# Decode layer on one core: a 128-row block of w4 moved to 16 partitions, its other rows in loads of 5, 4, 3 and 1

## The chip, the cores and the metric

The kernel runs on one NeuronCore of a Trainium2 chip. The metric is the device time of one execution in microseconds (us), the median over three runs; lower is better. All times in the text are microseconds unless marked ns. Positions such as 185.53 are counted from the start of the profiled span.

## The reference, cut to what matters

Eight tokens (B = 8, one step each, D = 512) go through two stages.

```python
# A: pre-norm attention, 32 query heads on 8 key/value heads, last W = 2048 cache positions
q = (layernorm(x) @ wq).reshape(B, 1, 32, 128)
p = softmax(q @ k_cache[:, :, -2048:].T * 128**-0.5)
h = x + (p @ v_cache[:, :, -2048:]).reshape(B, 1, 4096) @ wo
# B: on layernorm(h); the token shift is zero for one step, so only the MLP is left
x1 = layernorm(h)
h2 = h + x1 + gelu(layernorm(x1) @ w3) @ w4      # w3: 512 x 1792, w4: 1792 x 512
```

All inputs are bf16. The cache slices are 64 MiB, wq and wo 4 MiB each, w3 and w4 1.75 MiB each: the kernel reads 79.18 MB (million bytes) from HBM.

## The kernel before, in words

Every large load is issued by SyncE (SP) into one queue, in an order written out by hand: wq, 32 cache loads of 2 MB (16 for k, 16 for v) into the eight slots of `ring`, four loads of wo (1 MB each) into `wbig`, two of w3, four of w4. A cache load waits (on SP) until its slot is free: `taken[...]` is the last PE product that reads the slot. w3 goes to slot 0 and w4 to slot 1 of the ring. Each of these loads fills 128 partitions, one piece of memory per partition.

For each of the eight tokens and two halves of the heads, PE transposes the keys (L325), ScalarE and VectorE copy them out (L334, L336), PE makes the scores (L345), a softmax follows, and PE multiplies with the values (L445, L454). GpSimd (POOL) spreads the softmax over four head columns (L384). The attention output is reordered (L534 to L540) and multiplied by wo in four parts as the loads land (`pe_wo`, L548). `hd` (L685), the statistics (L687 to L699) and `uT` (L692) lead to the MLP.

The MLP works on 14 chunks of 128 rows of the hidden width. `pe_w3(half, ...)` (L710) makes `y_ps` in two halves of the contraction, one for each load of w3. VectorE scales it into `g_x` (L738), ScalarE makes `gT` by gelu (L741), in two groups of chunks: the first `FH` = 8, then 6. `pe_fin` (L747) starts the sum in `z_ps` with the residual, and `pe_w4` (L755) adds two products of 256 columns for each chunk, one for each half of the output, waiting for the load of w4 that holds the chunk:

```python
FH = 8
for r, sem in zip((8, 3, 2, 1), sem_w4):
    w4_chunks += [slice(f0 + i, f0 + 128 * r, r) for i in range(r)]
    dma(SP, w4_sb[:, lo:lo + r, :].rearrange("p r n -> p (r n)"),
        B_w4[f0:f0 + 128 * r, :].rearrange("(p r) n -> p (r n)", r=r), sem, w_free[1] if lo == 0 else None)
```

So a load with r rows per partition gives r chunks, and its wait stands ahead of the products of these chunks. Two copies out of `z_ps` (L775, L776) and the store (L779) end the program.

`stream(n)` puts n products of 512 columns on PE whose result nobody reads (L596); they stand between stages from the last values on. There are 21 of them: 4, 3, then 0, 4, 4, 1 behind the four parts of wo, then 2, 1 and 2.

Of the kernel before, what the change touches and what calls it, by code (L numbers as in the profile page):

```python
# [11 lines left out]
B = 8  # L12
D = 512
# [9 lines left out]
FC = F // 128  # L23
# [3 lines left out]
NS = 8  # L27
# [40 lines left out]
def bass_sequential_preLN__sliding_block_cached__mixer_s_mlp__decode_kernel(  # L68
# [23 lines left out]
    with es:  # L92
        sb = lambda shape, dtype, name: es.enter_context(nc.sbuf_tensor(name, shape, dtype))
        ps_t = lambda shape, dtype, name: es.enter_context(nc.psum_tensor(name, shape, dtype))
        S = lambda name: es.enter_context(nc.semaphore(name))
# [4 lines left out]
        ident_b = sb([128, 128], dt.bfloat16, "ident_b")  # L100
# [16 lines left out]
        QH, RW = H // 8, 8  # L117
# [4 lines left out]
        ring = sb([128, NS, NCQ * DH], dt.bfloat16, "ring")  # L122
        W3S, W4S = (2 * 2 * NB) % NS, (2 * 2 * NB + 1) % NS
        w3_sb = ring[:, W3S, 0:KC * F].rearrange("p (k f) -> p k f", k=KC)
        w4_sb = ring[:, W4S, 0:FC * D].rearrange("p (k n) -> p k n", k=FC)
# [4 lines left out]
        P4_sb = sb([128, 512, 4], dt.bfloat16, "P4_sb")  # L130
# [42 lines left out]
        gT = sb([128, FC * B], dt.bfloat16, "gT")  # L173
# [6 lines left out]
        kbank = [t[:, :].bitcast(dt.float32) for t in kT_ps]  # L180
# [10 lines left out]
        sem_wo = [S(f"sem_wo{i}") for i in range(NWO)]  # L191
        sem_x, sem_wq, sem_out = (S(n) for n in ("sem_x", "sem_wq", "sem_out"))
        sem_w3 = [S(f"sem_w3{i}") for i in range(2)]
        sem_w4 = [S(f"sem_w4{i}") for i in range(4)]
        PE, AC, DV, PO, SP = (Engine(S(n)) for n in ("s_pe", "s_act", "s_dve", "s_pool", "s_sp"))

        def dma(eng, dst, src, sem, *waits):
            def f(e):
                e.dma_start(dst, src).then_inc(sem, 16)  # L199
            eng.op(f, *waits, inc=False)  # L200
# [18 lines left out]
        e = DV.op(lambda e: e.bn_stats(st6[:, :], x_sb[:, :]), X)  # L219
        e = DV.op(lambda e: e.bn_aggr(mv[:, :], st6[:, :]), e)  # L220
        e = AC.op(lambda e: e.activation(rstd[:, :], mv[:, 1:2], ACT.Sqrt, bias=eps1[0:B, :], scale=1.0), e, e_eps)
        e = DV.op(lambda e: e.reciprocal(rstd[:, :], rstd[:, :]), e)
# [36 lines left out]
        e = PE.op(pe_xT, e_xln, e_idb)  # L259
# [22 lines left out]
        e = PE.op(pe_qT, *e_qr)  # L282
# [18 lines left out]
        place = {l: n for n, l in enumerate(quads)}  # L301
        taken = {}
# [6 lines left out]
        e_sp, e_max, e_mT, e_neg, e_negps, e_negc, e_exp, e_PT, e_pT, e_lsel, e_Lb, e_rL, e_scale = ({} for _ in range(13))  # L309
        NG = NB * 8  # L310
        NV = 2 * NB - 1
        LAST = NB - 1
# [174 lines left out]
        def pick_rest(w, *parts):  # L487
            for a in parts:
                pick_part(w, a, DV)
                if a == 3:  # L490
                    e_acc[w] = e_part[w]
# [51 lines left out]
        def pe_wo(n, *waits):  # L543
            def f(e):
                for q in range(n * (QH // NWO), (n + 1) * (QH // NWO)):
                    for r in range(RW):
                        for nb in range(KC):
                            ins = e.matmul(hT_ps[:, nb * NW:(nb + 1) * NW], wo_v[:, q, r, cols[nb]],  # L548
                                           oR_t[:, r * NW + q * B:(r + 1) * NW + q * B], start=(q == 0 and r == 0 and nb == 0),
                                           stop=(q == QH - 1 and r == RW - 1), skip_group_check=True)  # L550
                return ins
            e_wo.append(PE.op(f, (sem_wo[n], 16), e_exp[NB - 2], *waits))
# [4 lines left out]
        def pv(*quarters):  # L557
            for i in quarters:
                pe_PV(i)
                if i in at:  # L560
                    finish(at[i])
                if i == NG - 1:
                    scale(LAST, 1, S_ps[1][:, 0:16], e_PV[i])
# [29 lines left out]
        def stream(n):  # L593
            def f(e):
                for _ in range(n):
                    ins = e.matmul(O2_ps[:, :], ident_b[:, :], kT_sb[:, (NG - 1) % NKT, 0:512], start=True, stop=True)  # L596
                return ins
            if n:
                PE.op(f, e_acc[NV - 4])
# [37 lines left out]
        pick_rest(14, 1)  # L637
        finish(13)
        pick_rest(14, 2, 3)
        stream(4)  # L640
        pv(60)
        finish(14)
        pv(61, 62, 63)

        e_oR = reorder()
        stream(3)
        for n in range(NWO):
            pe_wo(n, e_oR, e_oz)
            stream((0, 4, 4, 1)[n])


        dma(SP, wq_v, A_wq.rearrange("(p k) n -> p k n", k=KC), sem_wq)
        for l in loads:
            what, b, j = l
            if what == "wo":
                n, qh = b, QH // NWO
# [4 lines left out]
            n = place[l]  # L661
# [4 lines left out]


        w_free = [taken[quads[n - NS]] for n in (len(quads), len(quads) + 1)]
        for a, sem in enumerate(sem_w3):
            dma(SP, w3_sb[:, 2 * a:2 * (a + 1), :].rearrange("p r f -> p (r f)"),  # L670
                B_w3[256 * a:256 * (a + 1), :].rearrange("(p r) f -> p (r f)", r=2), sem, w_free[0])

        FH = 8
        w4_chunks, w4_ends, f0 = [], [], 0
        for r, sem in zip((8, 3, 2, 1), sem_w4):
            lo = len(w4_chunks)
            w4_chunks += [slice(f0 + i, f0 + 128 * r, r) for i in range(r)]
            dma(SP, w4_sb[:, lo:lo + r, :].rearrange("p r n -> p (r n)"),
                B_w4[f0:f0 + 128 * r, :].rearrange("(p r) n -> p (r n)", r=r), sem, w_free[1] if lo == 0 else None)
            w4_ends.append(lo + r)  # L680
            f0 += 128 * r
        assert len(w4_chunks) == FC

        e_uz = PO.op(lambda e: e.memset(uT, 0.0), e_PT[LAST, 3])
        e_d = DV.op(lambda e: e.tensor_tensor(v3(hd[:, :]), hT, v3(xc[:, :]), ALU.add), e_wo[-1], e_xc[0])  # L685
# [5 lines left out]
        e_ms = DV.op(lambda e: e.tensor_reduce(msum[:, :], vr(st1), AX.X, ALU.add), e_st1)  # L691
        e_u = DV.op(lambda e: e.scalar_tensor_tensor(uT[:, :, 0:B], bc(msum), -1.0 / D, v3(hd[:, :]),  # L692
                                                     ALU.mult, ALU.add), e_ms, e_uz)
        stream(2)
        e_vs = DV.op(lambda e: e.tensor_reduce(vsum[:, :], vr(st2), AX.X, ALU.add), e_st2)
        e_m2 = DV.op(lambda e: e.tensor_tensor(msq[:, :], msum[:, :], msum[:, :], ALU.mult))
        e_vs = DV.op(lambda e: e.scalar_tensor_tensor(vsum[:, :], msq[:, :], -1.0 / D, vsum[:, :],
# [7 lines left out]
        def pe_w3(half, lo, hi, *waits):  # L705
            def f(e):
                for fc in range(lo, hi):
                    n, f = divmod(fc, FH)
                    for kc in (2 * half, 2 * half + 1):
                        ins = e.matmul(y_ps[n][:, f * NY[n]:(f + 1) * NY[n]], w3_sb[:, kc, w4_chunks[fc]],  # L710
                                       uT[:, kc, 0:NY[n]], start=(kc == 0 and f == 0), stop=(kc == KC - 1),
                                       skip_group_check=True)
                return ins
            return PE.op(f, *waits)
        pe_w3(0, 0, FC, e_u, (sem_w3[0], 16), e_scale[LAST, 1], e_acc[NV - 2])
        stream(1)
        e_y = [pe_w3(1, 0, FH, (sem_w3[1], 16)), pe_w3(1, FH, FC)]

        e = AC.op(lambda e: e.activation(s2[:, :], vsum[:, :], ACT.Sqrt, bias=eps2[:, :], scale=(1.0 + EPS) / D), e_vs)  # L719
        e1 = AC.op(lambda e: e.activation(s1[:, :], vsum[:, :], ACT.Sqrt, bias=eps1[:, :], scale=1.0 / D))  # L720
# [2 lines left out]
        e = DV.op(lambda e: e.reciprocal(r1[:, :], s1[:, :]), e1)  # L723
        e = DV.op(lambda e: e.tensor_tensor(v3(xb[:, :]), v3(hc[:, :]), bc(r1), ALU.mult), e, e_hc)
        e = DV.op(lambda e: e.tensor_tensor(xb[:, :], xb[:, :], hp[:, :], ALU.add), e)
        e = DV.op(lambda e: e.tensor_tensor(v3(fin[:, :]), hT, v3(xb[:, :]), ALU.add), e)
        e = DV.op(lambda e: e.tensor_copy(f_hi[:, :], fin[:, :]), e)
# [6 lines left out]
        e_gT = []  # L734
        for n in range(2):
            fn = (FH, FC - FH)[n]
            cs = slice(n * FH * B, (n * FH + fn) * B)
            e = DV.op(lambda e, n=n, cs=cs, fn=fn: e.tensor_tensor(v3(g_x[:, cs]),   # L738
                y_ps[n][:, 0:fn * NY[n]].rearrange("p (f w) -> p f w", w=NY[n])[:, :, 0:B], bcf(r2, fn),
                                                                   ALU.mult), e_y[n], e_r2)  # L740
            e_gT.append(AC.op(lambda e, cs=cs: e.activation(gT[:, cs], g_x[:, cs], ACT.Gelu_apprx_tanh), e))  # L741
        z_ps = S_ps[1]

        def rows(e, w, rhs, start=False, stop=False):
# [3 lines left out]
                               stop=stop, tile_position=(0, 64 * a), skip_group_check=True)  # L748
            return ins

        def pe_w4(lo, hi, *waits):
            def f(e):
                for fc in range(lo, hi):
                    for a in range(2):
                        ins = e.matmul(z_ps[64 * a:64 * a + B, 0:256], gT[:, fc * B:(fc + 1) * B],  # L755
                                       w4_sb[:, fc, 256 * a:256 * (a + 1)].rearrange("p (j r) -> p r j", r=2),
                                       start=False, stop=(fc == FC - 1), tile_position=(0, 64 * a), skip_group_check=True)
                return ins
            return PE.op(f, *waits)

# [4 lines left out]
            return ins  # L765

        PE.op(pe_fin, e_fin, e_exp[LAST], e_scale[LAST, 1])
        stream(2)
        for n, hi in enumerate(w4_ends):
            e_z = pe_w4(w4_ends[n - 1] if n else 0, hi, (sem_w4[n], 16), e_gT[0 if hi <= FH else 1])  # L770
        e_out = []
        for a in range(2):
            src = z_ps[64 * a:64 * a + B, 0:256].rearrange("p (r j) -> p r j", r=2)
            dst = out_sb[:, 256 * a:256 * (a + 1)].rearrange("p (j r) -> p r j", r=2)
# [38 lines left out]
```

## Time and profile before

| | us |
|---|---|
| median of 3 runs (193.53 to 193.57) | 193.54 |
| the profiled execution | 193.76 |
| its span, first to last instruction | 192.3 |
| PE busy | 159.8 |
| VectorE busy | 103.8 |
| ScalarE busy | 84.4 |
| GpSimd busy | 35.8 |

The profiled execution lies 0.22 above the median, and 1.46 of it lies outside the span. The granted TensorE clock of the core is 1.000. The instruction trace names the line, the tiles and the releaser of a wait; for the loads it also holds each packet (start, duration, bytes, queue) and the landing events of each load, one from each DMA engine that carried a part of it. The packets are not marked with their engine.

### The profile page before, as it was taken

To read this page: it belongs to the slowest core of one execution; us is meant where nothing else is said; L and a number is where in the kernel's file an instruction comes from. 1 tells how busy PE (TensorE), PEld (TensorE's weight loads), DVE (VectorE), ACT (ScalarE), POOL (GpSimd) and SP (SyncE) were. 2 spreads that over 40 slices of the span, in tenths; PEclk is the share of its full clock that TensorE was granted. 3 is DMA by queue.
4 is the path that set the end of the run, shared out by engine and by line. 5 is a ranking of instruction groups with operands and counts; after the bars stand their busy time and mean duration, and the time that the engine had idled before them with its cause. 6 is when DMAs were issued, how large, how long until landed. Compare 5 with 4: busy or idle time off the path is not lost.

```text
span 192.3 us, 4741 instructions
## 1 busy us (share of the span) xinstructions
PE 159.8 (83%) x2108; PEld 101.8 (53%) x2108; DVE 103.8 (54%) x256; ACT 84.4 (44%) x102; POOL 35.8 (19%) x44
## 2 busy tenths in 40 slices
PE   0028999789998989998999797979998998898795
PEld 0015767567665555655656464646565653366472
DVE  7702656367457654665475546554765456552050
ACT  5002776946744544454444532454445423530040
POOL 8000000350520080008000800052004402400000
PEclk9999999999999999999999999999999999999999
DMA  6999999999999999999999999999999999999992
GB/s 220 436 423 436 433 416 433 426 428 423 436 429 433 429 433 423 426 429 431 433 423 433 429 433 429 429 433 426 424 426 429 429 433 433 423 416 430 418 381 77
DMA packets 6244, 79.47 MB, mean 413 GB/s; under 512 B 705, under 2 KB 849, under 8 KB 1361
## 3 DMA queue, kind: packets, MB, share of 16 engines
q1 hardware_dynamic: 6208, 79.18, 97.0%
q8 instruction: 16, 0.26, 0.5%
q10 hardware_dynamic: 16, 0.01, 0.0%
q14 instruction: 4, 0.02, 0.0%
HBM read 79.18 MB, written 0.01 MB: 412 GB/s over the span
## 4 chain that ended last, share of the span: by engine, by line
DMA 78%; PE 16%; DVE 2%; SPq 2%; issue 1%; ACT 0%
DMA ring<-in_A_k_cache_dram 63%; DMA ring<-in_B_w_dram 16%; PE kT_ps L325 8%; PE O_ps L445 3%; PE S_ps L345 3%; SPq L199 2%; DVE kT_sb L336 1%; PE sm L394 1%; PE sm L496 1%; DVE pT_sb L407 1%; PE S_ps L755 0%; DVE mcol L356 0%; ACT P_sb L775 0%; PE sm L360 0%; PE sm L370 0%
## 5 line engine op out<-in xcount | busy, mean ns | idle before, releaser
L334 ACT ACTIVATE kT_sb<-kT_ps 128x1024 bf16<-128x1024 bf16 x64 | 65.2, 1023 | 65.4 <-PE kT_ps L325 65.4
L325 PE MATMUL kT_ps<-ident_p,ring 128*128 128x128 bf16 x1024 | 68.3, 220 | 9.0 <-DMA ring<-in_A_k_cache_dram 7.6
L336 DVE COPY kT_sb<-kT_ps 128x1024 bf16<-128x1024 bf16 x64 | 44.3, 692 | 48.9 <-PE kT_ps L325 48.9
L325 PEld LDWEIGHTS kT_ps<-ident_p,ring 128*128 128x128 bf16 x1024 | 57.7, 98 | 22.5 <-DMA ring<-in_A_k_cache_dram 10.5
L384 POOL TENSOR_TENSOR P_sb<-P_sb,mask_b 128x512 bf16<-128x512 bf16 x30 | 31.2, 1070 | 129.2 <-ACT P_sb L374 120.1
L445 PE MATMUL O_ps<-ring,pT_sb 128*64 128x512 bf16 x208 | 31.6, 390 | 0.0
L345 PE MATMUL S_ps<-kT_sb,qwin 128*32 128x512 bf16 x256 | 26.0, 390 | 0.0
L345 PEld LDWEIGHTS S_ps<-kT_sb,qwin 128*32 128x32 bf16 x256 | 6.8, 93 | 16.3 <-issue 14.4
L394 PE MATMUL sm<-ident_s,P_sb 128*128 128x128 bf16 x120 | 11.6, 219 | 2.0 <-DVE pT_sb L407 0.7
L407 DVE COPY pT_sb<-sm 128x512 bf16<-128x512 bf16 x28 | 11.6, 415 | 1.1 <-PE sm L394 1.1
L445 PEld LDWEIGHTS O_ps<-ring,pT_sb 128*64 128x64 bf16 x208 | 7.7, 108 | 6.1 <-issue 1.6
L394 PEld LDWEIGHTS sm<-ident_s,P_sb 128*128 128x128 bf16 x120 | 7.7, 97 | 4.5 <-issue 3.6
L480 DVE SCALAR_TENSOR_TENSOR acc<-O_ps,own_f,acc 128x128 f32<-128x128 f32 x24 | 8.4, 350 | 0.8
L268 PE MATMUL S_ps<-wbig,xlnT 128*32 128x512 bf16 x32 | 3.4, 596 | 5.3 <-DMA wbig<-in_A_wq_dram 5.3
L374 ACT ACTIVATE P_sb<-S_ps,negcol 128x512 bf16<-128x512 f32 x8 | 5.5, 687 | 3.0 <-DVE negcol L373 3.0
L254 PE MATMUL sm<-ident_b,xln_b 8*128 8x8 bf16 x4 | 0.3, 174 | 7.6 <-DVE xln_b L223 7.6
L496 PEld LDWEIGHTS sm<-sum_f,acc 128*128 128x128 f32 x20 | 3.0, 188 | 6.3 <-DVE pT_sb L407 3.3
L356 DVE TENSOR_REDUCE mcol<-S_ps 128x1 f32<-128x512 f32 x8 | 5.5, 689 | 1.5 <-PE S_ps L345 1.5
L480 DVE SCALAR_TENSOR_TENSOR iota_f<-O_ps,own_f,iota_f 128x128 f32<-128x128 f32 x15 | 5.2, 348 | 1.5 <-ACT iota_f L483 1.2
L596 PE MATMUL O_ps<-kT_sb,ident_b 128*128 128x512 bf16 x21 | 5.8, 379 | 0.0
L435 DVE TENSOR_TENSOR oT_all<-sm,rL 128x16 bf16<-128x16 f32 x15 | 3.4, 229 | 4.4 <-PE sm L496 4.3
L719 ACT ACTIVATE s<-vsum,eps 128x8 f32<-128x8 f32 x1 | 0.3, 301 | 11.8 <-DVE vsum L699 11.8
(123 smaller groups left out, 109.8 us busy)
## 6 DMA issues: line engine op xcount, KB each, us to landing
ring<-in_A_k_cache_dram SPq DMA_DIRECT2D x16, 2048.0 KB, 30.7
ring<-in_A_v_cache_dram SPq DMA_DIRECT2D x16, 2048.0 KB, 26.8
wbig<-in_A_wq_dram SPq DMA_DIRECT2D x1, 4096.0 KB, 12.3
wbig<-in_A_wo_dram SPq DMA_DIRECT2D x4, 1024.0 KB, 29.9
ring<-in_B_w_dram SPq DMA_DIRECT2D x2, 896.0 KB, 34.9
ring<-in_B_w_dram SPq DMA_DIRECT2D x1, 1024.0 KB, 32.1
ring<-in_B_w_dram SPq DMA_DIRECT2D x1, 384.0 KB, 30.3
ring<-in_B_w_dram SPq DMA_DIRECT2D x1, 256.0 KB, 30.5
```

The source lines that it names most:

```text
L325: ins = e.matmul(kT_ps[m % 3][:, c * 128:(c + 1) * 128], ring[:, s, n * DH:(n + 1) * DH], ident_p[:, :], is_transpose=True)
L334: e_lo[i] = AC.op(lambda e: e.activation(kT_sb[:, i % NKT, 0:1024], kT_ps[2 * i % 3][:, :], ACT.Copy), e_Tlo[i], e_QK.get(i - NKT))
L336: e_hi[i] = DV.op(lambda e: e.tensor_copy(kT_sb[:, i % NKT, 1024:2048], kT_ps[(2 * i + 1) % 3][:, :]), e_Thi[i], e_QK.get(i - NKT))
L345: ins = e.matmul(S_ps[b % 2][32 * h:32 * (h + 1), :], qwin[:, b, 4 * j + h, w0:w0 + 32], kT_sb[:, i % NKT, :].rearrange("p (c h k) -> p h ...
L356: e_max[b] = DV.op(lambda e: e.tensor_reduce(mcol[:, :], S_ps[b % 2][:, :], AX.X, ALU.max), e_QK[8 * b + 7], e_mT.get(b - 1))
L374: e_exp[b] = AC.op(lambda e: e.activation(P_sb[:, :], S_ps[j][:, :], ACT.Exp, bias=negcol[:, j:j + 1], scale=1.0, accum_out=lcol[:, j:j + 1]),
L384: e_sp[b, r] = eng.op(lambda e, r=r, pb=pb, mb=mb: e.tensor_tensor(P4_sb[:, 128 * r:128 * (r + 1), :], pb, mb, ALU.mult), e_exp[b], e_PT.g ...
L394: ins = e.matmul(buf[:, x * 128:(x + 1) * 128], P4_sb[:, 32 * c:32 * (c + 1), :].rearrange("p k h -> p (k h)"), ident_s[:, :], is_transpos ...
L407: e_pT[b, r] = DV.op(lambda e: e.tensor_copy(dst, pT_ps[:, :]), e_PT[b, r], free)
L445: ins = e.matmul(bank(w)[64 * t:64 * (t + 1), :], pT_sb[:, b % NB3, c, 64 * j:64 * (j + 1)], ring[:, s, :].rearrange("p (a c d) -> p c a d ...
L480: e_part[w] = eng.op(lambda e: e.scalar_tensor_tensor(dst, src, own, dst, ALU.mult, ALU.add), e_part[w], e_PV[4 * w + 3])
L596: ins = e.matmul(O2_ps[:, :], ident_b[:, :], kT_sb[:, (NG - 1) % NKT, 0:512], start=True, stop=True)
```

## The change: what it does, and the diff

The first 128 rows of w4 leave the tile `w4_sb`. Eight loads of 16 KB, each for two partitions (p and p + 4) with eight rows of w4 in each, put them into 16 partitions of a cleared block of 64 partitions, `near_sb`, in the slot of the last k load (slot 2). POOL clears this block (64 x 4096) and a second one (`near`, 128 x 512), and copies parts of the identity into the second. The eight loads wait for the first clearing and are issued ahead of w3 and w4. The other 1664 rows come in loads of 5, 4, 3 and 1 rows per partition (640, 512, 384 and 128 KB); `FH` becomes 6.

After the first group of `gT` is made, eight products (`pe_near`) take the 8 columns of chunk 0 and place row r of each partition's eight rows in the partitions of `near_sb`; VectorE copies the result out (`gn`), and 16 products of 256 columns add that block to `z_ps`, behind those of the load with 5 rows. The unread products go from 21 to 13: 3, 2, then 0, 2, 3, 0, then 1, 2 and 0.

```diff
+        sem_near = S("sem_near")
...
-        stream(4)
+        stream(3)
...
-        stream(3)
+        stream(2)
         for n in range(NWO):
             pe_wo(n, e_oR, e_oz)
-            stream((0, 4, 4, 1)[n])
+            stream((0, 2, 3, 0)[n])
...
         w_free = [taken[quads[n - NS]] for n in (len(quads), len(quads) + 1)]
+        side = ring[:, place["k", LAST, 1] % NS, :]
+        near_sb = side[0:64, 0:RW * D].rearrange("p (r n) -> p r n", r=RW)
+        near = side[:, RW * D:RW * (D + 64)].rearrange("p (r n) -> p r n", r=RW)
+        e_nz = PO.op(lambda e: e.memset(near_sb, 0.0), taken["k", LAST, 1])
+        e = PO.op(lambda e: e.memset(near, 0.0))
+        e_near = PO.op(lambda e: e.tensor_copy(near.rearrange("p r (g n) -> p g r n", g=2)[:, :, :, 0:8],
+                                               ident_b[:, :].rearrange("p (g n r) -> p g r n", g=2, r=RW)), e)
+        for n in range(RW):
+            p, f = 32 * (n // 4) + n % 4, 64 * (n // 4) + RW * (n % 4)
+            dst = near_sb[p:p + 5:4].rearrange("p r n -> p (r n)")
+            a = B_w4[f:f + RW, :]
+            dma(SP, dst, bass.AP(tensor=a.tensor, offset=a.offset, ap=[[4 * RW * D, 2], [1, RW * D]]), sem_near, e_nz)
         for a, sem in enumerate(sem_w3):
...
-        FH = 8
-        w4_chunks, w4_ends, f0 = [], [], 0
-        for r, sem in zip((8, 3, 2, 1), sem_w4):
+        w4_chunks, w4_ends, f0 = [slice(0, 128)], [], 128
+        for r, sem in zip((5, 4, 3, 1), sem_w4):
...
+        FH = w4_ends[0]
...
-        stream(2)
+        stream(1)
         e_vs = DV.op(lambda e: e.tensor_reduce(vsum[:, :], vr(st2), AX.X, ALU.add), e_st2)
...
         pe_w3(0, 0, FC, e_u, (sem_w3[0], 16), e_scale[LAST, 1], e_acc[NV - 2])
-        stream(1)
-        e_y = [pe_w3(1, 0, FH, (sem_w3[1], 16)), pe_w3(1, FH, FC)]
+        stream(2)
+        e_y = [pe_w3(1, 0, FH, (sem_w3[1], 16)), pe_w3(1, FH, FC, (sem_near, 16 * RW))]
...
+        gn_ps = kbank[1][0:64, 0:RW * B]
+        gn = P4_sb[0:64, 64:80, :].rearrange("p k h -> p (k h)")
+
+        def pe_near(e):
+            for r in range(RW):
+                ins = e.matmul(gn_ps[:, r * B:(r + 1) * B], near[:, r, :], gT[:, 0:B], start=True, stop=True)
+            return ins
...
         PE.op(pe_fin, e_fin, e_exp[LAST], e_scale[LAST, 1])
-        stream(2)
+        e = PE.op(pe_near, e_gT[0], e_near)
+        e_gn = DV.op(lambda e: e.tensor_copy(gn, gn_ps), e, e_PT[LAST, 3])
         for n, hi in enumerate(w4_ends):
-            e_z = pe_w4(w4_ends[n - 1] if n else 0, hi, (sem_w4[n], 16), e_gT[0 if hi <= FH else 1])
+            e_z = pe_w4(gT, w4_sb, w4_ends[n - 1] if n else 1, hi, (sem_w4[n], 16), e_gT[0 if n == 0 else 1])
+            if n == 0:
+                pe_w4(gn, near_sb, 0, RW, e_gn)
```

More of the change, by code (lines that the diff above doesn't have):

```diff
@@ L678, in bass_sequential_preLN__sliding_block_cached__mixer_s_mlp__decode_kernel @@
             dma(SP, w4_sb[:, lo:lo + r, :].rearrange("p r n -> p (r n)"),
-                B_w4[f0:f0 + 128 * r, :].rearrange("(p r) n -> p (r n)", r=r), sem, w_free[1] if lo == 0 else None)
+                B_w4[f0:f0 + 128 * r, :].rearrange("(p r) n -> p (r n)", r=r), sem, w_free[1] if lo == 1 else None)
             w4_ends.append(lo + r)
@@ L707, in f @@
                 for fc in range(lo, hi):
-                    n, f = divmod(fc, FH)
+                    n, f = (0, fc) if fc < FH else (1, fc - FH)
                     for kc in (2 * half, 2 * half + 1):
@@ L749, in rows, with pe_w4 @@
             return ins
-        def pe_w4(lo, hi, *waits):
+        def pe_w4(g, w, lo, hi, *waits):
             def f(e):
@@ L754, in f @@
                     for a in range(2):
-                        ins = e.matmul(z_ps[64 * a:64 * a + B, 0:256], gT[:, fc * B:(fc + 1) * B],
-                                       w4_sb[:, fc, 256 * a:256 * (a + 1)].rearrange("p (j r) -> p r j", r=2),
-                                       start=False, stop=(fc == FC - 1), tile_position=(0, 64 * a), skip_group_check=True)
+                        ins = e.matmul(z_ps[64 * a:64 * a + B, 0:256], g[:, fc * B:(fc + 1) * B],
+                                       w[:, fc, 256 * a:256 * (a + 1)].rearrange("p (j r) -> p r j", r=2),
+                                       start=False, stop=(w is w4_sb and fc == FC - 1), tile_position=(0, 64 * a), skip_group_check=True)
                 return ins
```

## The prediction

> **What bounds the kernel now.** I read the page first, then the chain of waits, then the last stage by windows and by time. The page gives the chain to the loads, nearly all of them in one queue; a second queue carries PE's instructions.
>
> ```profile
> q1 hardware_dynamic: 6208, 79.18, 97.0%
> q8 instruction: 16, 0.26, 0.5%
> ...
> DMA 78%; PE 16%; DVE 2%; SPq 2%; issue 1%; ACT 0%
> ```
>
> The end of the chain says what the finish hangs on: a load of w4 issued at 159.31 lands at 189.78, six products follow, then copy and store.
>
> ```profile
> 159.31 30.47 DMA ring<-in_B_w_dram
> 189.78 0.04 issue
> 189.82 0.61 PE S_ps L755 x6
> 190.43 0.02 issue
> 190.45 0.45 ACT P_sb L775
> ```
>
> The windows from 184 on (columns: stretch, its length, busy time of PE, PE's weight loads, DVE, ACT, POOL, clock, DMA share, GB/s) show that the queue does not run full to its end: from 187 on about half of the engines move anything.
>
> ```profile
> 184.00:186.00 2.00, 1.64 (x32) 1.34 (x31) 1.50 (x9) 1.78 (x3) 0.00 (x0) 1.00 0.98 405
> 186.00:187.00 1.00, 1.00 (x27) 0.97 (x27) 0.23 (x1) 0.00 (x0) 0.00 (x0) 1.00 0.81 323
> 187.00:188.00 1.00, 0.90 (x13) 0.29 (x14) 0.21 (x1) 0.50 (x2) 0.00 (x0) 1.00 0.59 227
> 188.00:189.00 1.00, 1.00 (x16) 0.61 (x16) 0.00 (x0) 0.00 (x0) 0.00 (x0) 1.00 0.50 185
> ```
>
> The landing events of the last load, one from each of 16 engines, say the same: seven between 186.67 and 187.43, one at 188.33, eight between 189.61 and 190.09. At wq (12.57 to 13.07) they lay within 0.51. Followed packet by packet (on one engine the next packet starts 3 to 5 ns before the last one's recorded end), eight engines carried two of the sixteen 16 KB instruction packets each, about 0.93 apiece; these are the eight late ones. The engine at 188.33 carried two 8 KB instruction packets. The loads end when the late eight do.
>
> The order of time on PE shows the slack that this leaves:
>
> ```profile
> 185.57 1.45 PE L710 MATMUL kT_ps<-P_sb,ring 128*128 128x64 bf16 x28 [0.36 <-DMA ring<-in_B_w_dram]
> 186.96 0.28 PE L747 MATMUL S_ps<-ident_b,f_hi 128*8 128x128 bf16 x4
> 187.07 0.28 PE L747 MATMUL S_ps<-ident_b,f_lo 128*8 128x128 bf16 x4
> 187.28 0.61 PE L596 MATMUL O_ps<-kT_sb,ident_b 128*128 128x512 bf16 x2
> 187.99 2.43 PE L755 MATMUL S_ps<-ring,gT 128*8 128x256 bf16 x28
> ```
>
> 28 products of w4 take 2.43, but the first 16 of them start within 0.80: a pair costs 0.114 and 14 pairs 1.6. The rest is waiting for loads.
>
> **The loads.** Packets of w4 took 307 ns for 8 KB, 121 for 3, 84 for 2, 46 for 1, so 37.3 ns per KB and 9 fixed: 5 KB is 195, 4 KB 158. An engine carries eight of each. Before: 8 x (307 + 121 + 84 + 46) = 4.46. After: 8 x (195 + 158 + 121 + 46) = 4.16. Every engine without the two-partition loads ends 0.30 earlier, and that is the gain of the last landing if nobody else becomes last. Packets of 335 ns among those of 121 made the latest engine 0.18 later than the next (190.09 against 189.91); if they stay away, up to 0.48.
>
> The 128 KB taken out come back as eight loads of two 8 KB packets. Loads of 8 rows (x, the output) posted 8 engine landings, those of 128 partitions 16, so two partitions should use two engines: each gets 8 x (307 + 9) = 2.53, net +2.23. Which two decides the sign. I assume that it is the same pair for all eight loads, and the first two, in the engines' order, of the eight that carried x. [...]
>
> If the pair is among the early seven, it ends at 186.67 to 187.43 plus 2.23, so at 188.9 to 189.66, ahead of the others' 189.79: hidden. w3 lands on it by 183.05 + 2.53 = 185.58, beside 185.53 now.
>
> **Issue.** On SP the eight loads wait for POOL's clearing, and behind them stand all six loads of w3 and w4, issued at 148.8 to 172.5 until now. POOL is free at 165.26 (L384); clearing 4096 elements, by 3.29 for 3840 (L213), takes 3.5: 168.8. Eight issues at 0.37 (output) to 0.58 (x) end by 173.5, six more at 0.43 by 176.1. The first engine needs new work at 178.0, when its part of the last wo load lands, and wq began to move 1.05 after its issue. w3, issued by 174, would move by 175.5: cost nothing, with 2.5 of cover; beyond that each microsecond counts in full. The added wait on `sem_near` (ahead of the second group's 16 products and all of PE's later work) is over by 183.8 on any engine (wo lands at 178.0 to 181.3, plus 2.53), ahead of 186.3. POOL's other two steps and the clearing of `uT` (0.31) end near 170.5; `uT` is needed at 183.28.
>
> **PE.** Twelve products (0.06 each) instead of 16 make the first group of `gT`: ready at 187.02 instead of 187.28. `pe_near`: no row has this shape; 32-column products of L710 follow each other at 25 ns, those of L534 at 13, so 0.1 to 0.2 of issue plus 0.18 to drain. I take 187.5. Copy of 64 columns: L685 0.19, L738 0.225; 187.75 with its hand-over. PE meanwhile does the five-row load (landing 185.53 + 1.54 = 187.07): 5 pairs, 187.9. The 16 products on `near_sb` are 8 pairs, 0.91: 188.8. Then 4 pairs, 189.26; the three-row load lands at about 189.27 to 189.5 and takes 0.34, the last one at 189.6 to 189.79. PE is there at 189.61. So 1.2 of added products is covered by the waits, with 0 to 0.2 to spare; what `pe_near` and the copy take beyond my values counts in full, since all later products of w4 stand behind `near_sb`'s on PE; at most 0.2 by these rows.
>
> **Unread products.** 21 become 13, at up to 0.22 each. They stood in waits: behind wo's parts PE waits 1.1 for loads in all. Removing them gives nothing. Their loss would cost something if the granted clock (1.00 in every window from 160 on) fell; at half clock the last 21 pairs alone would cost 2.4. The holes behind wo's parts grow from 0.35 and 0.75 by two and one products, to 0.8 and 1.0; PE waited up to 1.3 for keys and kept its clock, so nothing.
>
> **Sum.** -0.30 from the bytes, a few hundredths more for the slow packets: -0.34. The profiled execution lies 0.22 above the median; the difference goes on the median: 193.54 - 0.34 = 193.20; this case's own range is 193.0 to 193.45 (gain 0.48 and the scatter of the runs; 0.10 if the whole 0.2 of `pe_near` counts).
>
> **Rivals.**
> 1. *The pair is late already.* One of the two is among the eight that carry instruction packets: 190.09 - 0.30 + 2.53 = 192.32, so +2.23, 195.77. It decides as soon as the pair's lead over the last engine is under 2.23. Of the eight engines that carried x (call them 0 to 7), three carry such packets, one after the other in turn, so I read three neighbours among eight: two of six placements touch 0 or 1. For it: the trace numbers no engine. Against: with the four others before them in the turn and the one behind, the order fits 9 to 12, 5 to 7, 8, without a wrap past 15.
> 2. *One of the pair is the engine at 188.33.* It was among x's eight. Lead 1.76: +0.47, 194.01.
> 3. *The loads are spread over all 16 engines.* No bytes move between engines, the last landing stays, PE's extra work hides: 193.5. Against: the 8-row loads.
> 4. *Each two-partition load must finish before the next moves.* With the 0.9 that SP waits for the output's store, 8 x 0.94 = 7.5 on the pair: 186.7 to 187.4 + 7.5 - 0.3 = 194.6 at most, +4.5, 198. Against: the 128 KB load lands 0.31 behind its predecessor, its packets' time alone. [...]
>
> **How the numbers follow.** Forecast 0.57, late pair 0.17 (the count's one in three, less for the turn), the 188.33 engine 0.16, spread 0.07, one after the other 0.02, 0.01 for the rest. Leaving out the late pair and the string, the range is 193.0 to 194.2. A measurement of this kernel tells about 0.2% (0.39) from no change: faster means under 193.15. The forecast's 0.30 to 0.48 straddles that, a little over half of it beyond: 0.33. Same: the rest of it and the spread, 0.31. Slower: rivals 1, 2, 4 and the rest, 0.36.
>
> **What would show it.** Right: two landing events per two-partition load, both by 181.3; the last load's events end near 189.8, with two of the former early seven at 188.9 to 189.7; chain still load, products, copy; PE's wait ahead of the last two products short or gone. Wrong: w3's second load landing near 188 (rival 1); 16 events per small load (rival 3); a DMA share under 0.98 before 184 (issue too late); the clock under 1.00; products of `near_sb` ending after 189.3.

## The result, and the profile after

The changed kernel takes 194.12 (median of 8, 193.88 to 194.85) against 193.56 (193.46 to 193.68) for the kernel before, a ratio of 1.0034, interval 1.002 to 1.0049. It is slower by 0.56, where 0.34 faster was forecast. Runs more than 1.5% above the fastest of their kernel are left out of all medians in this text; there is one, of 198.42 in e4.

Two sums make this up. The profiled execution, the longest of the eight, took 194.85 with a span of 193.0. In the eight runs the span has a median of 192.35 and the time outside the span one of 1.78 (1.60 to 1.87); of the kernel before they are 192.2 and 1.33 (medians of the comparisons below). So of the 0.56 about 0.45 lies outside the span. In three of the eight runs the granted TensorE clock was 1.000, with spans of 192.1 to 192.3. The loads did what was forecast. These are the queues and the shares of the chain on the page of the kernel after:

```profile
q1 hardware_dynamic: 6240, 79.18, 96.7%
...
DMA 55%; PE 36%; DVE 4%; ACT 3%; SPq 1%; issue 1%
```

The same bytes in 32 packets more; but DMA has only 55% of the chain, PE 36% where it had 16%. These shares cover the whole kernel and move for other reasons too (67% DMA and 26% PE in e7, which is as fast as the kernel before), so the end of the chain has to be read. The end of the chain of waits of the kernel after (start, us, what):

```profile
181.41 1.04 PE S_ps L549 x32
...
184.21 1.11 PE kT_ps L723 x28
185.32 0.85 PE O_ps L597 x2
186.17 1.11 PE kT_ps L723 x28
188.32 2.75 PE S_ps L775 x40
```

After the last wo load, which lands at 181.4, no load stands in the chain. The end hangs on PE, which works through w3, two unread products (L597), w3 again and 40 of w4's products. The windows of the kernel after (stretch, length, PE, weight loads, DVE, ACT, POOL, clock, DMA share, GB/s) say why:

```profile
177.00:182.00 5.00, 3.35 (x88) 2.25 (x84) 0.00 (x0) 0.00 (x0) 0.00 (x0) 0.96 1.02 423
182.00:184.00 2.00, 1.72 (x22) 1.39 (x19) 0.94 (x6) 0.00 (x0) 0.00 (x0) 0.50 1.02 426
184.00:186.00 2.00, 2.00 (x32) 1.39 (x31) 1.52 (x11) 1.46 (x3) 0.00 (x0) 0.50 1.00 411
...
188.00:189.00 1.00, 1.00 (x19) 0.61 (x19) 0.22 (x1) 0.00 (x0) 0.00 (x0) 0.79 0.61 223
189.00:190.00 1.00, 1.00 (x20) 0.60 (x20) 0.00 (x0) 0.00 (x0) 0.00 (x0) 1.00 0.10 35
190.00:191.00 1.00, 1.00 (x18) 0.60 (x16) 0.00 (x0) 0.00 (x0) 0.00 (x0) 1.00 0.00 0
```

The third column from the right is the granted clock: half speed from 181.60 to 188.43, as the trace has it. From 184 on PE is busy all the time, and from 190 on no DMA engine moves anything while PE still has 1.07 to do. The order of time on PE shows the delay:

```profile
184.00 1.31 PE L723 MATMUL kT_ps<-P_sb,ring 128*128 128x64 bf16 x28
185.16 1.01 PE L597 MATMUL O_ps<-kT_sb,ident_b 128*128 128x512 bf16 x2
185.97 1.31 PE L723 MATMUL kT_ps<-P_sb,ring 128*128 128x64 bf16 x28
...
187.73 0.59 PE L760 MATMUL kT_ps<-gT,ring 128*64 128x8 bf16 x8
188.25 0.80 PE L775 MATMUL S_ps<-ring,gT 128*8 128x256 bf16 x10
188.98 1.07 PE L775 MATMUL S_ps<-ring,P_sb 64*8 64x256 bf16 x16
189.98 1.07 PE L775 MATMUL S_ps<-ring,gT 128*8 128x256 bf16 x16
```

The last product ends at 191.05, 0.6 later than before, although the last load landed at 189.80, 0.29 earlier (190.09 before). Single traces scatter here: over all that are kept, the last landing lies at 189.92 to 190.09 with the loads of before (before, e2, e6 and e9; mean 190.00) and at 189.54 to 189.91 with the eight small loads and the new split (after, e1, e5, e8 and e10 to e13; mean 189.71). Its 16 landing events came at 186.47 to 187.03 (five), 188.19 and 189.13 to 189.80 (ten); before they were seven, one and eight.

### The profile page after: what moved, and what is told of

It reads as the page before. It is cut to its first block, busy times and chain, and to the rows that moved or that the text cites. A ratio compares the mean times of both kernels' runs of the same rounds, so it can differ in the third digit from the quotient of the medians.

```text
span 193.0 us, 4781 instructions
## 1 busy us (share of the span) xinstructions
PE 161.2 (84%) x2122; PEld 104.2 (54%) x2122; DVE 104.0 (54%) x257; ACT 84.4 (44%) x102; POOL 40.1 (21%) x47
## 4 chain that ended last, share of the span: by engine, by line
DMA 55%; PE 36%; DVE 4%; ACT 3%; SPq 1%; issue 1%
DMA ring<-in_A_k_cache_dram 31%; DMA wbig<-in_A_wo_dram 17%; PE kT_ps L326 17%; DMA wbig<-in_A_wq_dram 6%; PE S_ps L346 5%; PE O_ps L446 4%; DVE kT_sb L337 2%; PE S_ps L269 2%; ACT kT_sb L335 2%; PE S_ps L775 1%; PE kT_ps L723 1%; SPq L200 1%; PE sm L395 1%; ACT L375 1%; PE O_ps L597 1%
## 5 line engine op out<-in xcount | busy, mean ns | idle before, releaser
L326 PE MATMUL kT_ps<-ident_p,ring 128*128 128x128 bf16 x1024 | 69.4, 222 | 7.5 <-DMA ring<-in_A_k_cache_dram 6.1
L326 PEld LDWEIGHTS kT_ps<-ident_p,ring 128*128 128x128 bf16 x1024 | 59.0, 99 | 20.7 <-DMA ring<-in_A_k_cache_dram 8.3
L549 PE MATMUL S_ps<-oR,wbig 128*128 128x32 bf16 x128 | 3.7, 179 | 2.3 <-DMA wbig<-in_A_wo_dram 1.7
```

Of the source, the lines that this page charges most:

```text
L326: ins = e.matmul(kT_ps[m % 3][:, c * 128:(c + 1) * 128], ring[:, s, n * DH:(n + 1) * DH], ident_p[:, :], is_transpose=True)
```

## The experiments

Each was run beside the kernel before (193.45 to 193.51 in these comparisons, span 192.1 to 192.2, 1.31 to 1.33 outside it). "Outside" is the median of the time less the span.

**The first theory:** the unread products that were taken out let the clock fall, and the added products (`pe_near` and those on `near_sb`) then had no slack left to hide it. **Rivals:** the added loads, or GpSimd's clearing in front of them, cost the time by themselves; or the added products do, at any clock.

**e1, the kernel after with seven unread products put back.** Against the kernel after:

```diff
-        stream(3)
+        stream(4)
-        stream(2)
+        stream(3)
-            stream((0, 2, 3, 0)[n])
+            stream((0, 4, 4, 1)[n])
...
-        stream(1)
+        stream(2)
```

> The changed kernel with the unread products ahead of w3 put back to the counts of before (4, 3, then 0, 4, 4, 1, then 2; the 2 and 0 behind w3 stay as changed), so 20 instead of 13. Clock theory (the removed products let the granted clock fall to half at about 181.6 and PE ends the kernel instead of the loads): clock 1.000 in all runs, last landing 189.8, PE waits for it again, time 193.2 to 193.4, under the kernel before. Rival, extra work on PE (the near products and the copy are themselves too long): clock 1.000 but PE still the last, 193.6 to 193.9. Rival, a cost that the span does not show (three runs of the changed kernel with clock 1.000 took 193.88 to 194.02 at spans of 192.1 to 192.3): span near 192.1 and time near 193.9.

193.58 (11 runs), ratio 1.0008 (0.9999 to 1.0017), span 192.0, outside 1.54. The clock was 0.999 or 1.000 in eight runs and 0.991 in three, where the expectation had 1.000 in all. The time is not the 193.2 to 193.4 of the theory but the lower end of the first rival's, in which PE is still the last; of this, 0.2 lies outside the span, where the second rival looked for the cost. In the profiled run the clock is full and the last load lands at 189.54; PE by time:

```profile
183.44 1.08 PE L723 MATMUL kT_ps<-P_sb,ring 128*128 128x64 bf16 x28
184.38 0.59 PE L597 MATMUL O_ps<-kT_sb,ident_b 128*128 128x512 bf16 x2
185.50 1.09 PE L723 MATMUL kT_ps<-P_sb,ring 128*128 128x64 bf16 x28 [0.53 <-DMA ring<-in_B_w_dram]
...
186.85 0.41 PE L760 MATMUL kT_ps<-gT,ring 128*64 128x8 bf16 x8
187.19 0.73 PE L775 MATMUL S_ps<-ring,gT 128*8 128x256 bf16 x10
187.86 1.07 PE L775 MATMUL S_ps<-ring,P_sb 64*8 64x256 bf16 x16
188.86 1.07 PE L775 MATMUL S_ps<-ring,gT 128*8 128x256 bf16 x16
```

The two unread products take 0.59 where they took 1.01, and leave PE 0.53 of waiting ahead of w3's second load. PE's last product ends 1.1 earlier. With the clock kept, the added products cost nothing that the span shows: it is 0.2 shorter than before. But PE waits for no load of w4 any more. The end of the chain of this run, without its small pieces, goes from w3's second load through PE alone:

```profile
174.12 11.34 DMA ring<-in_B_w_dram
...
185.50 1.09 PE kT_ps L723 x28
...
187.26 2.69 PE S_ps L775 x42
```

What pays for the added products on this path is that w3's second 28 products take 1.09 where they took 1.45 (see the last section).

**e2, the kernel before with the 13 unread products** (the lines of e1 the other way, and those behind w3 as in the change).

> The kernel before with the 13 unread products of the changed one (3, 2, then 0, 2, 3, 0, then 1, 2, 0), nothing else changed. Clock theory: the clock falls in some runs (mean 0.98 to 0.99) and these take up to 0.9 longer, since 14 pairs of w4 at half clock need 3.2 instead of 1.6; median 193.6 to 194.4. If the clock does not fall here, the near products or the holes of the changed kernel's end are part of the cause and the time stays at 193.5 to 193.6.

193.49, ratio 1.0 (0.9992 to 1.0009), span 192.2, outside 1.33. The clock fell in 9 of 11 runs and cost nothing: the part of the expectation that gave the fall a price was wrong. In the profiled run it was half from 183.70 to 187.11, and then the kernel before still waits for its loads:

```profile
187.28 0.28 PE L747 MATMUL S_ps<-ident_b,f_lo 128*8 128x128 bf16 x4
188.04 1.41 PE L755 MATMUL S_ps<-ring,gT 128*8 128x256 bf16 x22 [0.48 <-DMA ring<-in_B_w_dram]
189.63 0.62 PE L755 MATMUL S_ps<-ring,gT 128*8 128x256 bf16 x6 [0.18 <-DMA ring<-in_B_w_dram]
```

So neither half of the edit costs span alone; the two together do.

**e3, the kernel before with the clearing and the eight small loads, which nobody reads.**

> The kernel before with POOL's clearing of 64 x 4096 and the eight two-partition loads added, their data unread (128 KB read twice); all loads of w4 and all unread products as before. Pair early (the forecast): two of the early engines end 2.53 later, at 189.2 to 190.0, the last landing stays at about 190.1, time 193.5 to 193.6. Pair late: the last landing moves to 192.6, time 196. A cost of the loads or the waits outside the span: time 193.8 to 194.0 at an unchanged span.

193.83, ratio 1.0018 (1.0009 to 1.0027), span 192.3, last landing 189.87: the small loads hide. But the time rose by 0.35, of which 0.2 is outside the span (1.52).

**e4, e1 with two loads of eight partitions in place of eight loads of two.**

```diff
-        for n in range(RW):
...
+        for n in range(2):
+            dma(SP, near_sb[32 * n:32 * n + 8].rearrange("p r n -> p (r n)"),
+                B_w4[64 * n:64 * (n + 1), :].rearrange("(p r) n -> p (r n)", r=RW), sem_near, e_nz)
```

> e1_more_stream with the same 128 rows brought to the same 16 partitions by two loads of 8 partitions, so eight engines with 16 KB each instead of two with 64 KB. If three of these eight are among the late ones, they get 2 x 316 ns = 0.63: last landing 0.63 behind that of e1_more_stream, about 190.4, time up to 0.6 over e1_more_stream. If none of them is late, it equals e1_more_stream. If the number of small loads costs time of its own, it is faster than e1_more_stream.

196.1 (four runs), ratio 1.0129 (1.0106 to 1.0152), span 194.1, last landing 191.46. Far worse than any case of the expectation. From 178.0 to 179.5, 23 packets of 8 KB take 400 to 755 ns, against 309 for 8 KB in the loads of w4 before; the small loads have 16 packets, so others are wo's. Until 183.0, 79 packets of 7 KB (w3's) take over 300 ns (one in e1), against 272, and the last of the 16 landings of the small loads comes at 183.50. The DMA share stays at 1.04, but less gets through: from 178.10 to 179.50 the windows show 250 GB/s here and 441 in e1. Why such packets are slow was not tested.

**The second theory:** what lies outside the span grew too, and GpSimd's clearing, not the loads, is behind it. e5 to e8 take the parts singly.

**e5, the kernel after once more**, for the same comparison.

> The changed kernel once more, on one chip with the next three. In the first job its span was 192.1 to 193.0 (kernel before in the second job: 192.0 to 192.3) and its time lay 1.6 to 1.9 above its span (kernel before 1.3, e1_more_stream 1.54). Two parts expected: a span 0.2 to 0.8 longer than that of e1_more_stream (191.9 to 192.3), longest where the clock is lowest, and 0.2 or more outside the span. If it comes out at 193.5 the difference to e1_more_stream was the chip's.

194.63 (6 runs), ratio 1.0056 (1.004 to 1.0071), span 192.9, outside 1.83. The granted clock was 0.982 in five runs, with spans of 192.8 to 193.0, and 1.000 in one, with 192.0 and 193.84. Over all 14 runs of the kernel after, the span has a median of 192.9 with a clock of 0.982 (seven runs) and of 192.1 with 1.000 (four): half a clock for 6.8 costs about 0.8.

**e6, the kernel before with the clearing alone**, w3's issue waiting for it.

> The kernel before with POOL's clearing of 64 x 4096 and w3 and w4 waiting for it on SP, no small loads. If the 0.2 outside the span of e3_loads_only (time minus span 1.53 against 1.33) comes from the late issue or from POOL, it is here too: 193.7 at a span of 192.15. If it comes from the small loads: 193.5, 1.33 outside the span.

193.72, ratio 1.0012 (1.0003 to 1.002), span 192.2, outside 1.52.

**e7, the kernel before with the eight loads alone**, no clearing.

> The kernel before with the eight two-partition loads (unread) straight behind the last transposes, without POOL's clearing, so issued 9 to 11 us earlier. If the loads cost the 0.2 outside the span: 193.7 to 193.8, as e3_loads_only. If the clearing does: 193.5.

193.49, ratio 0.9999 (0.9991 to 1.0008), span 192.2, outside 1.31. Issued this early, the loads cost nothing; behind the clearing they add no more than 0.1 (193.83 in e3, 193.72 in e6). The clearing costs 0.2, none of it in the span.

**e8, e1 without the clearing of `near_sb`.**

> e1_more_stream without the clearing of near_sb: the other 48 partitions keep finite keys, which meet zeros in gn, so the output is the reference's. Span as e1_more_stream, 191.95 (last landing 189.55, 0.3 to 0.5 ahead of the kernel before). If the clearing or the late issue makes the 0.2 outside the span: 193.3, faster than the kernel before by 0.2. If the loads make it: 193.5 to 193.6, no different.

193.62, ratio 1.001 (1.0001 to 1.0018), span 191.9, outside 1.69. The clearing's own work is not it: two GpSimd steps are left, and the time outside is no shorter than in e1 (1.54). That it is 0.15 longer stays open.

**e9, the kernel before with one small GpSimd step.**

```diff
+        PO.op(lambda e: e.memset(scratch[:, 0:1], 1.0), e_warm)
         e_uz = PO.op(lambda e: e.memset(uT, 0.0), e_PT[LAST, 3])
```

> The kernel before, with one more GpSimd step: a one-column memset of the scratch tile, ahead of the clearing of uT. If any added GpSimd step of that place costs the 0.2 us that the clearing alone cost outside the span (1.31 to 1.52 us), the time is about 193.7 us, with 1.5 outside the span. If it was the 3.5 us of the clearing, or the wait of w3's issue for it, this is the kernel before: 193.5 us, 1.3 outside the span.

193.7, ratio 1.001 (1.0001 to 1.0019), span 192.2, outside 1.52. One column is enough: 0.2 comes with the added step, not with its 3.5 us of work.

**e10, e8 with the table filled by VectorE**, so that GpSimd has no added step.

```diff
-        e = PO.op(lambda e: e.memset(near, 0.0), e_nz)
-        e_near = PO.op(lambda e: e.tensor_copy(near.rearrange("p r (g n) -> p g r n", g=2)[:, :, :, 0:8],
+        e = DV.op(lambda e: e.memset(near, 0.0), e_nz)
+        e_near = DV.op(lambda e: e.tensor_copy(near.rearrange("p r (g n) -> p g r n", g=2)[:, :, :, 0:8],
```

> The kernel after with the unread products restored, near_sb not cleared, and the table near filled by VectorE behind fin's low half and not by GpSimd, so that GpSimd has no added step. This leaves out the clearing of near_sb. If the time outside the span grows with added GpSimd steps, it is 1.3 here, and with a span of 191.9 the time is 193.2 us, faster than before by 0.3. If it grows with the program's size, or with the table and its eight products wherever they are made, it stays at 1.5 to 1.7 and the time is 193.5 to 193.6.

193.3 (12 runs), span 192.0, outside 1.32: the first case, 0.2 below the kernel before. But three runs took 194.31 to 194.41 (outside 2.3 in two, a span of 193.1 in one), the other nine 193.18 to 193.60, and the interval of the ratio, 0.9989 to 1.0018, holds 1. One run each with 2.2 and 2.3 outside stands in e1 (194.13) and e8 (194.22) too; in the 115 runs of the kernel before the most is 1.46. What makes these runs is open.

**e11, the kernel after with only the products behind wo's parts put back.**

> The kernel after with only the unread products behind wo's parts restored (0, 4, 4, 1; 18 in all), those ahead of wo and behind the statistics left at the fewer. If the clock falls because of the holes behind wo's parts, it stays at 1.00 and the span is 192.0 us, the time 193.7 to 193.8. If the holes ahead of wo or behind the statistics (182 us) decide, the clock falls as in the kernel after: 0.982, a span of 192.9, 194.6 us.

193.58, ratio 1.001 (1.0002 to 1.0019), span 192.0, outside 1.55. The clock was 0.999 or 1.000 in eight of 11 runs, against four of the 14 runs of the kernel after. So the holes behind wo's parts make most of the difference; the first case holds in the main, though the clock still fell in three runs, as it did in three of e1. In its three runs with a clock of 0.982 or 0.991 the span was 192.3 to 192.5.

**e12, e10 with `uT` cleared by VectorE too**, one GpSimd step fewer than before.

> The kernel of e10 with the clearing of uT moved from GpSimd to VectorE too, which is idle there for 6.5 us, so that GpSimd has one step fewer than in the kernel before. near_sb is not cleared here either. If the time outside the span goes by the number of GpSimd's steps (1.31 before, 1.52 with one more), it is about 1.1 here; with e10's span of 192.0 the time is 193.1 us. If an added step costs but a removed one gives nothing, it is 1.3 and 193.3 us. If a repeat of e10's three runs of 194.3 to 194.4 is part of this form, some of these runs lie there too.

193.27 (12 runs), ratio 0.9997 (0.9986 to 1.0008), span 191.9, outside 1.34. The second case: a step taken away gives nothing back. Runs of 194.08 and 194.20 occur here too (outside 2.0 and 2.4).

**e13, the kernel after without GpSimd's added steps**, the table by VectorE, `near_sb` not cleared, 13 unread products.

> The kernel after, with its 13 unread products, but without GpSimd's three added steps: near_sb is not cleared (this part is left out), the table near is filled by VectorE. The clock falls to half at about 181.7 as in the kernel after, so the span is 192.9 us where it lasts 6.8 us and 192.0 to 192.5 where it does not. If the whole growth of the time outside the span (1.31 to 1.83 in the kernel after) is GpSimd's added steps, it is 1.3 here: 193.3 to 194.2 us. If the fewer unread products bear a part of it (the kernel after with 20 of them had 1.54), it is 1.5 to 1.6: 193.5 to 194.5.

193.79 (11 runs), ratio 1.0014 (1.0005 to 1.0023), span 192.2, outside 1.52: the second case. With the added products, taking out the unread ones lengthens the time outside the span by 0.2 (1.32 in e10, 1.52 here), though in e2, without the added products, it did not (1.33). How a shorter list of instructions does this stays open.

### When the clock falls

Every stretch of full or half clock that these traces hold whole is a multiple of 3.413 us: 6.827 in the kernel after, 3.413 in e2 and e4, 160.426 (47 of them) before the fall. In these traces the clock thus changed on a grid of 3.413, and where that grid lies against the kernel differs from run to run (the falls came at 181.60 in the kernel after, 181.79 in e5, 183.70 in e2). A fall is nothing new: the kernel before had a clock of 0.991 or less in 25 of 115 runs, and these took on the whole no longer than the others (median 193.45 against 193.51); where in the kernel it fell there is not known. Cut along each run's own grid, the windows ahead of a fall are these, of the kernel after, e5, e2, e13 and e4 in turn (the second column is the length, the third PE's busy time):

```profile
178.19:181.60 3.41, 1.81 (x42) 1.20 (x43) 0.00 (x0) 0.00 (x0) 0.00 (x0) 1.00 1.01 417
```

```profile
178.38:181.79 3.41, 2.08 (x53) 1.47 (x54) 0.00 (x0) 0.00 (x0) 0.00 (x0) 1.00 1.02 421
```

```profile
180.29:183.70 3.41, 2.07 (x40) 1.54 (x40) 0.94 (x6) 0.00 (x0) 0.00 (x0) 1.00 1.01 423
```

```profile
180.00:183.41 3.41, 2.18 (x39) 1.49 (x38) 0.66 (x4) 0.00 (x0) 0.00 (x0) 1.00 1.00 414
```

```profile
182.64:186.05 3.41, 2.25 (x39) 1.49 (x36) 2.18 (x14) 1.23 (x3) 0.00 (x0) 1.00 1.02 417
```

And the same stretch where the clock was kept, of e1, e6 and the kernel before:

```profile
178.24:181.65 3.41, 2.31 (x54) 1.55 (x54) 0.00 (x0) 0.00 (x0) 0.00 (x0) 1.00 1.02 424
```

```profile
180.35:183.76 3.41, 2.27 (x40) 1.49 (x40) 0.87 (x6) 0.00 (x0) 0.00 (x0) 1.00 0.98 414
```

```profile
180.03:183.44 3.41, 2.61 (x42) 1.55 (x40) 0.73 (x5) 0.00 (x0) 0.00 (x0) 1.00 1.01 422
```

From 170 on, up to the window in which PE's work ends, the clock fell behind windows with 1.81 to 2.25 us of PE work and stayed behind those with 2.27 or more, about two thirds of the window. One window there lies on the wrong side, e13's from 173.17 to 176.58, with 2.23, after which the clock stayed. Earlier in the same traces the line does not hold. These two windows, of e2 and the kernel before, hold a wait for keys of 1.48 and 1.25, and the clock stayed:

```profile
115.43:118.84 3.41, 1.83 (x28) 1.28 (x28) 2.16 (x8) 0.38 (x1) 0.00 (x0) 1.00 1.02 437
```

```profile
115.17:118.58 3.41, 2.06 (x27) 1.20 (x28) 2.61 (x8) 0.52 (x2) 0.00 (x0) 1.00 1.00 428
```

Such windows with 1.83 to 2.15 stand in seven of the traces. So PE's busy time alone does not tell the windows ahead of a fall from the others. The windows that kept the clock hold products of 512 and 128 columns, those ahead of the falls mostly narrow ones (32 and 64 columns, wo's and w3's); whether that is what counts was not tested. The half-speed windows held more: one with 3.13 was followed by another in the kernel after, one with 2.91 in e5; the full clock came back behind one with 3.13 in e13, with 3.34 in e4, and with 3.41 or 3.42, the whole window, in the other three cases. That the lengthened products of a half clock count as busy time is part of this (28 products of w3 took 1.31 in the kernel after and 1.08 in e1). All this is read from windows; what runs show is that with the products put back the clock is mostly kept (0.999 or 1.000 in eight of 11 runs of e1 and in eight of 11 of e11, against four of the 14 of the kernel after). PE was busy for 53 to 66% of the window that preceded a fall (1.81 to 2.25 of 3.41), so the clock fell behind windows that were far from empty.

## Why the prediction was wrong

- **Loads: right.** -0.30 was forecast for the last landing, -0.29 measured, in this pair of traces and between the means of all kept ones. Two of the early seven landing events moved to the late group, hidden as forecast; that the pair is the first two of the eight engines that carried x was the author's assumption, and no run shows the order of the engines. Rivals 1 to 4 did not occur (no event after 189.80, two landings for each small load, all by 181.23). On each of the two engines the small loads landed about 0.31 apart, which is the time of one 8 KB packet (309 ns) and not the 0.94 for each load of rival 4.
- **Issue: right.** The eight loads were issued from 168.9 to 174, w3 at 174.0, the last of w4 by 176.8 (176.1 forecast); the DMA share stays at 0.99 to 1.02 from 170 to 186. The loads themselves cost no more than 0.1 (e3, e6, e7).
- **PE: right in the number at full clock, by two errors that cancel.** In e1 the last pair starts at 189.65 (189.61 forecast) and the products on `near_sb` end at 188.93 (188.8 forecast). The first group of `gT` was ready at 186.65, not 187.02, because w3's second 28 products took 1.09 and not 1.45. From there to the products of the five-row load it took 0.54, where 0.3 was forecast (187.9 less five pairs, less 187.02), and at each of the two changes between `gT` and `gn` PE lost 0.09. None of the "0 to 0.2 to spare" was left: after w3's second load PE does not wait again, and the last load (189.54) is there before PE. With w3 at 1.45 that run would end some 0.36 later, at about 190.3 (an estimate from these figures), where the kernel before ends PE's work at 190.43.
- **Unread products: wrong, and the failed step.** The prediction saw the holes grow to 0.8 and 1.0 (they came out at 0.83 and 0.82), named the fall of the clock, and wrote "so nothing", because PE had waited up to 1.3 for keys and kept its clock. The comparison was false. In the kernel after the clock fell to half in ten of 14 runs (in the profiled one behind a grid window that holds both holes), and with the products behind wo's parts put back it was kept in eight of 11 (e11). A window with a wait for keys kept the clock at 2.06 of PE work, windows around wo's parts lost it at 2.07 and 2.08 (e2, e5): a hole among the keys was no measure for a hole here. What in the work makes the difference stays open. The price that it named for the half clock, 2.4, was too high: about 0.8 measured, since the fall ends at 188.4 and part of it goes into waits.
- **Sum: a second step failed.** "The difference goes on the median" takes the time outside the span to stay. It rose from about 1.33 to 1.78 and 1.83: 0.2 for an added GpSimd step (e9), 0.2 with the fewer unread products (e13), the rest open. Of the 0.92 between 194.12 and the forecast, about half lies here and half in the span (192.35, where 192.2 - 0.34 = 191.86 was forecast). Even the runs with the clock kept took 193.84 to 194.02 with spans of 192.0 to 192.3. So without the clock's fall the forecast of a gain would have failed as well: with the clock kept the span is some 0.2 shorter, and this takes more. With both causes taken out (e10) the median is 193.30, near the 193.20 forecast; as w3's shorter products have a part in that, the nearness is partly luck.
- **Rival 2** names nearly the measured time (194.01), by a mechanism that did not occur.

## What to carry to other kernels

Before unread or idle-looking TensorE work is removed, look at TensorE's work in every stretch as long as the clock's grid (3.4 us here), wherever the grid may lie; a check hole by hole is not enough. Compare such a stretch only with others of the same kind of products: waits that the clock survived elsewhere in the kernel proved nothing here (2.06 of PE work kept it among the keys, 2.07 and 2.08 around wo's parts did not). Then look at the clock of several runs, since the same program kept it in some and lost it in others (four and ten of 14). The half clock cost nothing in e2 (193.49), where PE still waited for its loads, and about 0.8 of the span in the kernel after, where it did not; so an edit that fills the last waits and one that lets the clock fall can each be free in the span and be dear together. Where some tenths of a microsecond are at stake, look at time less span as a result of its own (1.33 before, 1.78 after).

## What was not expected of the hardware

- One added one-column memset on GpSimd lengthened the execution by 0.2 outside the span (1.31 to 1.52 in e9); removing one step gave nothing (1.32 in e10, 1.34 in e12).
- Two loads of eight partitions (e4) were dearer than eight of two (e1): 8 KB packets of up to 755 ns instead of 309, and 2.5 in time (196.1 and 193.58).
- 28 products of w3 took 1.46 before and 1.08 in e1, both at full clock. The split of w4 sets from which columns of w3 a chunk's weights are read: side by side, or every second to eighth one. Chunk by chunk, the weight loads of 128 x 128 in these two traces took 95 to 99 ns at a step of 1 or 2 columns, about 103 at 3, 118 at 4, 131 at 5 and 157 to 165 at 8 (the first loads of a group aside; side by side it was 96 with 64 moving columns and with 32), with products following every 25 to 29, 25 to 28, 33, 40 and 60 ns. Before, eight of the 14 chunks had a step of 8; now the largest is 5.
